# Two alternating tiles for the blocks to be inverted, in the room of a tile of ones and a score tile

## The chip, the cores and the metric

The kernel runs on one core of one Trainium2 chip. The metric is the device time in microseconds (us) of one execution; the time of a kernel is the median over its runs. A core has five engines that run side by side: TensorE (PE in the rows; its weight loads are PEld), VectorE (DVE), ScalarE (ACT), GpSimd (POOL) and SyncE (SP), whose queue issues most DMAs. Each takes its own instructions strictly in the order in which the kernel put them, and waits on semaphores for the others.

## The reference, cut to what matters

```python
for t in range(S):                                   # S = 768 steps, state [B=4, H=8, 40, 40]
    y[:, :, t] = einsum('bhd,bhde->bhe', rt, state)
    Sa = einsum('bhde,bhe->bhd', state, at)
    state = state * wt - einsum('bhd,bhe->bhde', Sa, bt) + einsum('bhd,bhe->bhde', vt, kt)
...
mixed = real(fft(fft(x, axis=1), axis=2)); u = x + mixed           # x: y as [4, 768, 320]
u = u + relu(norm(u) @ w_ch1) @ w_ch2                              # 1280 wide
u = u + (relu(u.T @ w_tok1) @ w_tok2).T                            # over the sequence, 256 wide
out = u + relu(u @ w_ch1') @ w_ch2'                                # 1536 wide
```

A recurrence over 768 steps of 32 heads comes first, then a Fourier mixing and three two-layer networks. The weights are held in 64 bits and are decoded to a high and a low part on the chip.

## The kernel before, in words

The recurrence is cut into 12 windows of 64 steps (`NSC=768//L`). For each window i these stages are built, each a method of `Attn`:

- `load`, `decay`: the decays `wS` come in; a backward scan on DVE writes `Q` (L262), a reciprocal writes column 0 of `D2` (L264), and a forward scan with `D2` writes `R` (L265). `Q` is one tile, `R` has five. The backward scan takes a second tile, `D1`, which is zero but for a column of ones and is written once, in `init`. `D2` is zero too, but for its column 0, which the reciprocal fills anew in each window. POOL (in the first windows DVE) then multiplies `bt` and `a` and copies the last column of `R` (L268).
- `kg`: matmuls of the scaled keys give `RT` (four tiles). The diagonal 32x32 blocks of `RT` go to DRAM (`Gd<-RT`) and come back with the blocks of heads on partitions (`N<-Gd`): the even window of a pair fills partitions 0 to 63 of `N`, the odd one 64 to 127. There is one tile `N`.
- `inv`: once for two windows, DVE inverts all 128 triangular blocks in some forty dependent steps from `N` into `Mt`, with `MT` as scratch: the first step is a copy of the diagonal band (L333), the last reads of `N` are the products for the off-diagonal half (L331, `pr<-N,MT`), and the last step is a transposed copy to `MT` (L353). `Mt` and `MT` go to DRAM (`Md`, `Ad`).
- `merge`: the inverses come back (`AT<-Ad`, four times `Mst<-Md` for each window), and PE joins the halves (`mg`, `mc`) into `Mst`.
- `kbts`, `pts`, `load2`, `load3`: transposes of `bt` and `R`, and loads of v and r.
- `chain`: the recurrence over windows. PE products `x` (L424) from `RT` and the state `LT`, copied to `bdX`; products `z` (L436) with the inverse `Mst`; products `s` (L448), from which DVE and POOL (L452, L454) form the next state.
- `outp`: the output of the window. Six score groups: `sc` matmuls (L486), a copy to one of four score tiles `sc[k%4]` with a triangle mask (on DVE for k = 0, 2, 4; on ACT and POOL else), and the `y` matmuls (L504, L508) from it.

`wdec`, `decode` and `job` decode weights beside this. `out_tile` closes the room of `wS`, `Q`, `D1`, `D2`, `N`, `Mt`, `MT` and others and opens the tile `X` in it, which the Fourier stage `fft` reads; `fft2` and the networks (`ch`, `tok`, `tok2`) follow.

No order is written by hand. Each operation is given to a planner (`Plan.op`) with an engine, a guessed cost and the keys it reads and writes; from the keys come its dependences (a write waits for earlier reads and writes of the key). `Plan.emit` walks the operations in guessed time and, on each engine, takes of those that are ready the one with the smallest due time. Due times come from the guessed costs of the followers and from `OFF`, a table of offsets by stage and by stage and window. So a change of tiles or offsets may give every engine and SP's queue another order. Where a PE operation begins later than PE is free, and the planner's count of columns of the last 3.41 us is under `FILL[1]`, `fill` puts `warm` matmuls (L52) into the gap, whose result nobody reads.

Of the kernel before, what the change touches and what calls it, by code (L numbers as in the profile page):

```python
# [15 lines left out]
ALU = mybir.AluOpType  # L16
# [3 lines left out]
NG,NH,D,L=11,33,40,64  # L20
# [3 lines left out]
NBT,NR,NA,NRT=4,5,2,4  # L24
# [155 lines left out]
class Attn:  # L180
    def __init__(s,tc,ident,A,xd,ctx,pctx,xstack,tstack,T1d,W):
        s.tc=tc; s.nc=nc=tc.nc; s.ident=ident; s.A=A; s.xd=xd; s.xstack=xstack; s.tstack=tstack; s.T1d=T1d; s.W=W; s.X=None
        s.late=ExitStack(); s.mid=ExitStack(); s.early=ExitStack()
        e=s.late.enter_context(tc.tile_pool(name="a_e",bufs=1,side="right"))
        c=ctx.enter_context(tc.tile_pool(name="a_c",bufs=1))
# [70 lines left out]
    def decay(s,i):  # L256

        nc=s.nc; P=s.P; W=NG*(L+1)
        w=s.wS[i%2].rearrange("p g t -> p (g t)"); Q=s.Q[0]; R=s.R[i%NR]; D1=s.D1.rearrange("p g t -> p (g t)")
        D2=s.D2[0]; a=s.a[i%NA]; bt=s.bt[i%NBT]  # L260
        kw,kR,ka=('wS',i%2),('R',i%NR),('a',i%NA)
        P.op('DVE',1.84,lambda: nc.vector.tensor_tensor_scan(out=Q[:,W-1::-1],data0=w[:,W-1::-1],data1=D1[:,W-1::-1],initial=1.0,op0=ALU.mult,op1=ALU.add),[kw,'D1','Qe'],['Q'])  # L262
        PL=view(Q,1,[L+1,NG],[1,1])
# [24 lines left out]
    def kg(s,i):  # L288
        nc=s.nc; P=s.P; RT=s.RT[i%NRT]; bt=s.bt[i%NBT]
        am,kam=(s.am,'am') if i!=1 else (s.rm,'rm')  # L290
# [18 lines left out]
        R=i//2  # L309
# [4 lines left out]
        x=i%2  # L314
        s.dma(s.N[64*x:64*x+64],s.Gd[R%2][x].rearrange("b n j t -> (b n) j t"),[('Gd',R%2,x,b) for b in range(2)],[('N',x)],.85)


    def inv(s,R):
        nc=s.nc; V=nc.vector; P=s.P
        N2=s.N.rearrange("p a b -> p (a b)"); M2=s.Mt.rearrange("p a b -> p (a b)"); T2=s.MT.rearrange("p a b -> p (a b)")  # L320
# [144 lines left out]
    def outp(s,i):  # L465
# [16 lines left out]
        for k in range(6):  # L482
            gs=(k,k+6) if k<5 else (k,); m=len(gs); hs=s.psum('m',[128,512],"sc"); ks=('ps',hs[0]); j=k%4; t=s.sc[j]
            def f(gs=gs,hs=hs):
# [95 lines left out]
    def plan(s):  # L580
# [25 lines left out]
BL=2.761166073747128  # L606
OFF={'chain': -53.3, 'dec2': -42.2, 'decay': -47.7, 'decode': -65.8, 'fft': 52.7, 'fft2': -1.1, 'inv': 6.1,
     'kbts': -59.8, 'kg': -24.1, 'load': 23.5, 'load2': -12.5, 'load3': 57.3, 'loada': 23.1, 'merge': 4.3,
     'mlp': 83.4, 'out_tile': 104.0, 'outp': -27.8, 'pad': 107.3, 'pts': -24.7, 'tok': -208.8, 'tok2': -94.1,
     'wdec': -17.2, ('chain', 0): 52.1, ('chain', 1): -108.0, ('chain', 10): -36.6, ('chain', 11): 111.0, ('chain', 2): 26.3, ('chain', 3): 24.5,  # L610
     ('chain', 4): -27.4, ('chain', 5): 26.9, ('chain', 6): -31.5, ('chain', 7): 39.7, ('chain', 8): -97.4, ('chain', 9): -149.0, ('dec2', 0): 44.3,
     ('decay', 0): -79.2, ('decay', 1): 225.9, ('decay', 10): 52.5, ('decay', 11): -192.4, ('decay', 2): -350.0, ('decay', 3): 97.8, ('decay', 4): -8.0,
     ('decay', 5): -93.2, ('decay', 6): -36.4, ('decay', 7): -67.6, ('decay', 8): -26.7, ('decay', 9): 92.1, ('decode', 0): -15.0, ('fft', 0): 16.4,
     ('fft', 1): -226.4, ('fft', 2): -45.0, ('fft', 3): -150.0, ('fft2', 0): 17.0, ('fft2', 1): -24.7, ('fft2', 2): 34.9, ('fft2', 3): -36.4,
     ('inv', 0): 29.0, ('inv', 1): -35.3, ('inv', 2): -129.2, ('inv', 3): 6.5, ('inv', 4): -75.1, ('inv', 5): -3.6, ('kbts', 0): 21.2,
     ('kbts', 1): -16.2, ('kbts', 10): 101.1, ('kbts', 11): 40.4, ('kbts', 2): -47.2, ('kbts', 3): -102.5, ('kbts', 4): -141.5, ('kbts', 5): 81.5,
     ('kbts', 6): -102.5, ('kbts', 7): -63.4, ('kbts', 8): 26.3, ('kbts', 9): -73.0, ('kg', 0): -9.0, ('kg', 1): -49.8, ('kg', 10): -36.2,
     ('kg', 11): -191.3, ('kg', 2): 37.3, ('kg', 3): 95.7, ('kg', 4): 190.6, ('kg', 5): 19.9, ('kg', 6): -18.3, ('kg', 7): -91.4,
     ('kg', 8): -12.7, ('kg', 9): 21.0, ('load', 0): -74.7, ('load', 1): -11.2, ('load', 10): -128.8, ('load', 11): 53.3, ('load', 2): -92.0,
     ('load', 3): -31.7, ('load', 4): -86.8, ('load', 5): -25.2, ('load', 6): -288.2, ('load', 7): -85.8, ('load', 8): 56.2, ('load', 9): 109.9,  # L620
# [9 lines left out]
     ('outp', 8): 1.7, ('outp', 9): -65.6, ('pad', 0): 58.5, ('pts', 0): 27.8, ('pts', 1): -33.5, ('pts', 10): -26.1, ('pts', 11): -101.8,  # L630
     ('pts', 2): -149.3, ('pts', 3): 24.6, ('pts', 4): -146.2, ('pts', 5): 12.1, ('pts', 6): -66.4, ('pts', 7): -19.1, ('pts', 8): 33.0,
     ('pts', 9): -40.2, ('tok', 0): -61.9, ('tok', 1): -97.3, ('tok', 2): -41.9, ('tok', 3): 162.9, ('tok2', 0): 278.2, ('tok2', 1): 127.9,
     ('tok2', 2): -107.6, ('tok2', 3): -16.7, ('wdec', 0): -7.2}
# [43 lines left out]
class Mlp:  # L677
# [354 lines left out]
D2=(-60.0,1.0)  # L1032
# [56 lines left out]
```

## Time and profile before

| | us |
|---|---|
| median of 3 runs | 1023.37 (1022.95 to 1035.03) |
| the profiled execution's own time | 1029.61 |
| its span, first to last instruction | 1027.9 |
| PE busy in the span | 993.2 (97%) |
| DVE, ACT, POOL busy | 635.6, 422.8, 339.8 |

The profile is of one execution. A row of `--windows` kind gives the busy time of each engine in a stretch and the granted TensorE clock as a share of full speed: 1.00 is 2.4 GHz, 0.50 is 1.2 GHz. A row of the timeline gives start, duration, engine, line and operation, with the idle time before it and what ended that in square brackets. PE's busy time holds the `warm` matmuls, and its matmuls are pipelined, so that a busy PE is not PE at its peak.

### The profile page before, as it was taken

The numbers are of one execution on the slowest core, as the hardware profiler recorded it, in microseconds if no ns is written. First come the engines' busy times: TensorE is split into PE (matmuls) and PEld (weight loads), VectorE is DVE, ScalarE is ACT, GpSimd is POOL, SyncE is SP. The second block draws the span as 40 slices with busy tenths as digits, with TensorE's granted clock in tenths as the row PEclk, the third lists the DMA queues.
The fourth block names the chain that finished last, engine by engine and source line by source line (L and its number), as shares of the span: only waits on it lengthen the run. The fifth ranks groups of instructions, "written<-read, shape, count | busy, mean of one in ns | idle before, by whom it ended". The sixth has DMA issues, their size and how long they took to land.

```text
span 1027.9 us, 24475 instructions
## 1 busy us (share of the span) xinstructions
PE 993.2 (97%) x10135; PEld 951.4 (93%) x10135; DVE 635.6 (62%) x1346; ACT 422.8 (41%) x870; POOL 339.8 (33%) x425
## 2 busy tenths in 40 slices
PE   8898999899999999899999999999999999999998
PEld 8897888787888988899999999999999999999998
DVE  7598589788978539797888885334432432332322
ACT  4256587686766755342343422223221221221221
POOL 8584377668754544302344434100000000000000
PEclk9999699999999999899999999999999999999999
DMA  9986596989877887822454545900000000000000
GB/s 209 196 169 149 132 210 144 183 183 218 185 177 163 229 236 217 276 66 68 146 158 158 166 142 162 377 1 1 1 20 1 20 1 20 20 1 20 20 21 19
DMA packets 140722, 125.51 MB, mean 122 GB/s; under 512 B 100867, under 2 KB 118275, under 8 KB 140483
## 3 DMA queue, kind: packets, MB, share of 16 engines
q1 hardware_dynamic: 135811, 100.29, 39.6%
q0 software_dynamic: 4800, 23.67, 6.7%
q8 instruction: 79, 1.29, 0.6%
q14 instruction: 32, 0.26, 0.1%
HBM read 85.40 MB, written 33.75 MB: 116 GB/s over the span
## 4 chain that ended last, share of the span: by engine, by line
PE 73%; DVE 14%; DMA 6%; issue 2%; POOL 2%; SPq 2%; ACT 1%; DVEq 0%; POOLq 0%; ACTq 0%
PE hps L917 22%; PE acc L907 21%; DVE pr L331 4%; PE warm L52 4%; PE sc L486 3%; PE mix L851 3%; PE psA L824 2%; PE kg L297 2%; PE t2ps L994 2%; PE tps L981 2%; DMA Mst<-Md 2%; PE y L508 2%; SPq L217 1%; PE trp L888 1%; PE x L424 1%
## 5 line engine op out<-in xcount | busy, mean ns | idle before, releaser
L920 DVE SCALAR_TENSOR_TENSOR hl<-hps,hh 128x384 fp32r<-128x384 f32 x176 | 97.8, 556 | 239.0 <-ACT hh L919 238.4
L919 ACT ACTIVATE hh<-hps 128x384 fp32r<-128x384 f32 x176 | 86.4, 491 | 306.9 <-PE hps L917 306.9
L917 PE MATMUL hps<-th,v 128*128 128x384 f32 x576 | 143.0, 338 | 0.0
L907 PE MATMUL acc<-v,hh 128*128 128x320 f32 x576 | 129.5, 311 | 0.0
L917 PE MATMUL hps<-th,W 128*128 128x384 f32 x480 | 119.7, 339 | 0.9 <-DVE th L893 0.6
L907 PE MATMUL acc<-W,hh 128*128 128x320 f32 x480 | 107.9, 311 | 0.0
L52 PE MATMUL warm<-ident 128*128 128x128 f32 x760 | 101.5, 288 | 5.4 <-DVE A L833 3.4
L917 PEld LDWEIGHTS hps<-th,v 128*128 128x128 f32 x576 | 103.8, 188 | 0.2
L52 PEld LDWEIGHTS warm<-ident 128*128 128x128 f32 x760 | 96.2, 202 | 6.6 <-issue 3.5
L907 PEld LDWEIGHTS acc<-v,hh 128*128 128x128 f32 x576 | 97.6, 188 | 0.0
L785 POOL TENSOR_TENSOR mda<-mda,mdh 128x320 f32<-128x320 f32 (+2 forms) x44 | 44.4, 1009 | 153.9 <-ACT mdh L782 111.0
L917 PEld LDWEIGHTS hps<-th,W 128*128 128x128 f32 x480 | 86.8, 188 | 2.5 <-DVE th L893 1.0
L907 PE MATMUL acc<-v,hl 128*128 128x320 f32 x288 | 89.0, 309 | 0.0
L907 PEld LDWEIGHTS acc<-W,hh 128*128 128x128 f32 x480 | 80.8, 188 | 0.0
L907 PE MATMUL acc<-W,hl 128*128 128x320 f32 x240 | 74.0, 308 | 0.0
L917 PE MATMUL hps<-tl,v 128*128 128x384 f32 x192 | 64.6, 337 | 0.0
L307 POOL TENSOR_SCALAR_AFFINE_SELECT RT<-RT 64x384 f32<-64x384 f32 x72 | 52.6, 756 | 33.7 <-ACT RT L219 32.3
L297 PE MATMUL kg<-am,bt 120*128 120x192 f32 x242 | 52.2, 352 | 8.0 <-issue 2.6
L486 PE MATMUL sc<-rm,VZd 120*128 120x192 f32 x264 | 57.0, 350 | 2.1 <-DMA VZd<-in_vR_dram 1.0
L907 PEld LDWEIGHTS acc<-v,hl 128*128 128x128 f32 x288 | 54.1, 188 | 0.0
L917 PE MATMUL hps<-tl,W 128*128 128x384 f32 x160 | 53.9, 337 | 0.0
L496 POOL TENSOR_SCALAR_AFFINE_SELECT sc<-sc 64x384 f32<-64x384 f32 (+1 forms) x72 | 44.0, 612 | 27.3 <-ACT sc L219 24.7
(175 smaller groups left out, 2090.7 us busy)
## 6 DMA issues: line engine op xcount, KB each, us to landing
bt<-in_bkR_dram SPq DMA_DIRECT2D x12, 660.0 KB
mdraw<-in_moe_w_ch_dram SPq DMA_DIRECT2D x22, 320.0 KB
wS<-in_wR_dram SPq DMA_DIRECT2D x12, 335.2 KB
a<-in_aR_dram SPq DMA_DIRECT2D x12, 335.2 KB
RT<-a SPq DMA_DIRECT2D x36, 111.7 KB
LT<-in_vT_dram SPq DMA_DIRECT2D x12, 330.0 KB
VZt<-in_vT_dram SPq DMA_DIRECT2D x12, 330.0 KB
r<-in_rR_dram SPq DMA_DIRECT2D x12, 330.0 KB
```

The lines of the kernel that those rows point to most:

```text
L52: for x in range(m): nc.tensor.matmul(t[:,128*(x%4):128*(x%4)+128],lhsT=ident,rhs=ident,start=True,stop=True)
L297: nc.tensor.matmul(ps[:,192*x:192*x+192],lhsT=bt[:,g+x].rearrange("p v t -> p (v t)"),rhs=am[:,:,g+x],start=True,stop=True)
L307: nc.gpsimd.affine_select(out=kv,in_=kv,pattern=[[0,3*m],[1,L]],compare_op=ALU.is_gt,fill=0.0,base=0,channel_multiplier=-1)
L331: P.op('DVE',.16+.0012*st[0]*shape[0],lambda: V.tensor_tensor(out=pr,in0=a,in1=b,op=ALU.mult),rd,[('pr',h)])
L486: for x,g in enumerate(gs): nc.tensor.matmul(ps[:,192*x:192*x+192],lhsT=VZd[:,g].rearrange("p v t -> p (v t)"),rhs=s.rm[:,:,g],start=True, ...
L496: nc.gpsimd.affine_select(out=o,in_=o,pattern=[[0,3*m],[1,L]],compare_op=ALU.is_gt,fill=0.0,base=0,channel_multiplier=-1)
L785: P.op('POOL',.06+d*.0028,lambda: nc.gpsimd.tensor_tensor(out=g("da").bitcast(F32),in0=g("da").bitcast(F32),in1=g("dh").bitcast(F32),op=AL ...
L851: nc.tensor.matmul(s.pst(h)[:,:320],lhsT=aa[:K,sl],rhs=T2[:K,tb],start=n==0,stop=n==7)
L907: nc.tensor.matmul(s.pst(acc[x]),lhsT=a[:,sl],rhs=t[w2][w][:,m],start=(m==0 and n==0),stop=(m==MT-1 and n==2))
L917: for n,(l,r) in enumerate(ops): nc.tensor.matmul(ps,lhsT=l,rhs=r,start=n==0,stop=n==7)
L919: s.act(384,lambda: nc.scalar.activation(out=t["hh"][z],in_=s.pst(h),func=AF.Relu),[kp],[('hh',z)],free=[h[0]])
L920: s.dve(.47,lambda: nc.vector.scalar_tensor_tensor(out=t["hl"][z],in0=s.pst(h),scalar=0.0,in1=t["hh"][z].bitcast(F32),op0=ALU.max,op1=ALU. ...
```

## The change

`D1` goes. The backward scan reads `D2` instead, and before it in each `decay` POOL sets the column 0 of `D2` to one: 12 small memsets, in place of one memset of a whole tile and one of a column in `init`. Since the reciprocal and the forward scan of a window use the same column, the memset of window i+1 waits for the forward scan of window i, and the backward scan of window i+1 waits for the memset. `N` becomes two tiles, used in turn by the pairs of windows (`R%2`), so that the loads of a pair no longer wait for the reads of the pair before. The score tiles become three (`k%3`). The offsets `OFF` are changed in about a third of their entries, and `FILL[1]` rises from 9558.7 to 10345.2. `Gd`, `Md`, `Ad` had two tiles each and keep them; `Mt` and `MT` stay single.

```diff
-        s.D1,=mk(e,1,[120,NG,L+1],"D1"); s.D2=mk(e,1,[120,NG,L+1],"D2")
+        s.D2=mk(e,1,[120,NG,L+1],"D2")
-        s.N,=mk(e,1,[128,32,32],"N"); s.Mt,=mk(e,1,[128,32,32],"Mt"); s.MT,=mk(e,1,[128,32,32],"MT")
+        s.N=mk(e,2,[128,32,32],"N"); s.Mt,=mk(e,1,[128,32,32],"Mt"); s.MT,=mk(e,1,[128,32,32],"MT")
-        s.ys,=mk(c,1,[128,720],"ys"); s.sc=mk(c,4,[128,6,L],"sc")
+        s.ys,=mk(c,1,[128,720],"ys"); s.sc=mk(c,3,[128,6,L],"sc")
...
     def init(s):
-        s.zero(s.D1,['D1'],.63); s.one(s.D1[:,:,0:1],['D1'])
...
     def decay(s,i):
-        P.op('DVE',1.84,lambda: nc.vector.tensor_tensor_scan(out=Q[:,W-1::-1],data0=w[:,W-1::-1],data1=D1[:,W-1::-1],...),[kw,'D1','Qe'],['Q'])
+        s.one(D2[:,:,0:1],['D2']); D1=D2.rearrange("p g t -> p (g t)")
+        P.op('DVE',1.84,lambda: nc.vector.tensor_tensor_scan(out=Q[:,W-1::-1],data0=w[:,W-1::-1],data1=D1[:,W-1::-1],...),[kw,'D2','Qe'],['Q'])
...
-        s.dma(s.N[64*x:64*x+64],s.Gd[R%2][x].rearrange("b n j t -> (b n) j t"),[('Gd',R%2,x,b) for b in range(2)],[('N',x)],.85)
+        s.dma(s.N[R%2][64*x:64*x+64],s.Gd[R%2][x].rearrange("b n j t -> (b n) j t"),[('Gd',R%2,x,b) for b in range(2)],[('N',R%2,x)],.85)
...
-        NK=[('N',0),('N',1)]
+        NK=[('N',R%2,0),('N',R%2,1)]
...
-            ...; ks=('ps',hs[0]); j=k%4; t=s.sc[j]
+            ...; ks=('ps',hs[0]); j=k%3; t=s.sc[j]
...
-OFF={'chain': -53.3, 'dec2': -42.2, 'decay': -47.7, 'decode': -65.8, 'fft': 52.7, 'fft2': -1.1, 'inv': 6.1,
+OFF={'chain': -53.3, 'dec2': -42.2, 'decay': -47.7, 'decode': -65.8, 'fft': 43.0, 'fft2': -1.1, 'inv': 24.4,
...
-     ('inv', 0): 29.0, ('inv', 1): -35.3, ('inv', 2): -129.2, ('inv', 3): 6.5, ('inv', 4): -75.1, ('inv', 5): -3.6, ('kbts', 0): 21.2,
+     ('inv', 0): 29.0, ('inv', 1): -35.3, ('inv', 2): -149.9, ('inv', 3): -17.3, ('inv', 4): -75.1, ('inv', 5): -3.6, ('kbts', 0): 21.2,
...
-FILL=(0.22,9558.7)
+FILL=(0.22,10345.2)
```

## Rows read from the trace of the kernel before

**Rows 1.** Busy time by stage: us, PE, PEld, DVE, ACT, POOL, clock, DMA share, GB/s.

```profile
0.00:445.00 445.00, 415.21 (x6409) 376.88 (x6410) 346.14 (x669) 270.35 (x529) 263.33 (x339) 0.96 0.81 193
445.00:1028.00 583.00, 577.95 (x3728) 574.54 (x3727) 289.43 (x678) 152.50 (x342) 76.50 (x86) 1.00 0.21 68
```

**Rows 2.** The same stages, the `warm` matmuls alone: PE and PEld busy.

```profile
0.00:445.00 445.00, 98.09 (x737) 93.07 (x738) 0.96 0.81 193
350.00:400.00 50.00, 10.98 (x78) 10.14 (x78) 0.97 0.92 260
```

**Rows 3.** Chain of waits near window 10: start, us, what.

```profile
346.96 1.09 PE x L424 x32
...
348.76 12.13 DMA Mst<-Md
...
366.10 1.26 PE z L436 x32
```

**Rows 4.** SP's queue in the same stretch, timeline.

```profile
348.76 0.96 SPq L217 DMA_DIRECT2D Mst<-Md  x2
356.52 0.35 SPq L778 DMA_DIRECT2D mdraw<-in_moe_w_ch_dram  x1
357.42 0.46 SPq L217 DMA_DIRECT2D Mst<-Md  x1
```

**Rows 5.** Busy time and clock around a fall of the clock, columns as rows 1.

```profile
100.00:105.00 5.00, 3.56 (x48) 2.92 (x48) 4.86 (x11) 0.71 (x2) 4.32 (x6) 0.79 0.78 190
105.00:120.00 15.00, 15.00 (x177) 12.76 (x178) 9.95 (x21) 5.96 (x11) 2.54 (x6) 0.50 0.49 139
```

**Rows 6.** POOL's groups by shape: busy us, mean ns, idle before.

```profile
L268 POOL COPY R<-Q 120x11 f32<-120x11 f32 x10 | 3.5, 349 | 2.5 <-DVE R L265 2.3
...
L221 POOL MEMSET D<- 120x715 f32 x2 | 1.4, 694 | 0.0
...
L223 POOL MEMSET D<- 120x11 f32 x1 | 0.1, 113 | 0.0
```

**Rows 7.** DVE timeline: the first backward scan, and the one that waited for POOL.

```profile
4.34 1.65 DVE L262 TENSOR_TENSOR_SCAN Q<-wS,D 120x715 f32<-120x715 f32 x1 [4.34 <-DMA wS<-in_wR_dram]
...
25.94 1.65 DVE L262 TENSOR_TENSOR_SCAN Q<-wS,D 120x715 f32<-120x715 f32 x1 [1.04 <-POOL R L268]
```

**Rows 8.** DVE timeline: first copies of inversions 1 and 5, end of inversion 4.

```profile
83.44 0.57 DVE L333 COPY Mt<-N 128x4 f32<-128x4 f32 x1 [3.48 <-DMA Ad<-MT]
...
271.93 1.15 DVE L331 TENSOR_TENSOR pr<-N,MT 128x512 f32<-128x512 f32 x1
...
284.03 1.38 DVE L353 COPY MT<-Mt 128x1024 f32<-128x1024 f32 x1
...
299.56 0.17 DVE L333 COPY Mt<-N 128x4 f32<-128x4 f32 x1 [1.66 <-DMA N<-Gd]
```

**Rows 9.** SP's queue: the loads of N for inversion 5.

```profile
273.82 0.48 SPq L217 DMA_DIRECT2D N<-Gd  x1
...
287.96 1.02 SPq L217 DMA_DIRECT2D Gd<-RT  x2
...
293.36 0.95 SPq L217 DMA_DIRECT2D N<-Gd  x1
```

**Rows 10.** PE timeline: scores and outputs of windows 2, 3 and 11.

```profile
162.98 0.55 PE L508 MATMUL y<-kbt,sc 128*64 128x40 f32 x12 [1.25 <-DVE sc L491]
...
189.51 1.57 PE L486 MATMUL sc<-rm,VZd 120*128 120x192 f32 x8
191.01 0.43 PE L504 MATMUL y<-Sbd,r 120*64 120x120 f32 x4
...
398.10 0.50 PE L508 MATMUL y<-kbt,sc 128*64 128x40 f32 x12
398.53 1.57 PE L486 MATMUL sc<-rm,VZd 120*128 120x192 f32 x8
```

More of the change, by code (lines that the diff above doesn't have):

```diff
@@ L258, in decay @@
         nc=s.nc; P=s.P; W=NG*(L+1)
-        w=s.wS[i%2].rearrange("p g t -> p (g t)"); Q=s.Q[0]; R=s.R[i%NR]; D1=s.D1.rearrange("p g t -> p (g t)")
+        w=s.wS[i%2].rearrange("p g t -> p (g t)"); Q=s.Q[0]; R=s.R[i%NR];
         D2=s.D2[0]; a=s.a[i%NA]; bt=s.bt[i%NBT]
         kw,kR,ka=('wS',i%2),('R',i%NR),('a',i%NA)
-        P.op('DVE',1.84,lambda: nc.vector.tensor_tensor_scan(out=Q[:,W-1::-1],data0=w[:,W-1::-1],data1=D1[:,W-1::-1],initial=1.0,op0=ALU.mult,op1=ALU.add),[kw,'D1','Qe'],['Q'])
+        s.one(D2[:,:,0:1],['D2']); D1=D2.rearrange("p g t -> p (g t)")
+        P.op('DVE',1.84,lambda: nc.vector.tensor_tensor_scan(out=Q[:,W-1::-1],data0=w[:,W-1::-1],data1=D1[:,W-1::-1],initial=1.0,op0=ALU.mult,op1=ALU.add),[kw,'D2','Qe'],['Q'])
         PL=view(Q,1,[L+1,NG],[1,1])
@@ L482, in outp @@
         for k in range(6):
-            gs=(k,k+6) if k<5 else (k,); m=len(gs); hs=s.psum('m',[128,512],"sc"); ks=('ps',hs[0]); j=k%4; t=s.sc[j]
+            gs=(k,k+6) if k<5 else (k,); m=len(gs); hs=s.psum('m',[128,512],"sc"); ks=('ps',hs[0]); j=k%3; t=s.sc[j]
             def f(gs=gs,hs=hs):
@@ L538, in out_tile @@
         nc=s.nc; P=s.P; f=XW//2
-        keys=['D1','Q','D2',('N',0),('N',1),'m8','Mt','MT','dec']+[(v,x) for v in ('t1','m16','pr') for x in range(2)]+[(v,x) for v in ('t2','m32') for x in (0,4,8,10,12,14)]+['mt1','mt2']+[('wS',x) for x in range(2)]+[('a',x) for x in range(NA)]+[('am',h) for h in range(3)]
+        keys=['Q','D2']+[('N',y,x) for y in range(2) for x in range(2)]+['m8','Mt','MT','dec']+[(v,x) for v in ('t1','m16','pr') for x in range(2)]+[(v,x) for v in ('t2','m32') for x in (0,4,8,10,12,14)]+['mt1','mt2']+[('wS',x) for x in range(2)]+[('a',x) for x in range(NA)]+[('am',h) for h in range(3)]
         def close():
@@ new lines @@
+OFF={'chain': -53.3, 'dec2': -42.2, 'decay': -47.7, 'decode': -65.8, 'fft': 43.0, 'fft2': -1.1, 'inv': 24.4,
+     'kbts': -59.8, 'kg': -24.1, 'load': 23.5, 'load2': -12.5, 'load3': 57.3, 'loada': 16.2, 'merge': 4.3,
+     'mlp': 107.2, 'out_tile': 91.3, 'outp': -27.8, 'pad': 107.3, 'pts': -18.5, 'tok': -208.8, 'tok2': -104.1,
+     'wdec': -17.2, ('chain', 0): 52.1, ('chain', 1): -108.0, ('chain', 10): -36.6, ('chain', 11): 111.0, ('chain', 2): 26.3, ('chain', 3): 9.5,
+     ('chain', 4): -112.3, ('chain', 5): 26.9, ('chain', 6): -31.5, ('chain', 7): 39.7, ('chain', 8): -97.4, ('chain', 9): -149.0, ('dec2', 0): 44.3,
+     ('decay', 0): -79.2, ('decay', 1): 225.9, ('decay', 10): 52.5, ('decay', 11): -201.9, ('decay', 2): -346.1, ('decay', 3): 117.7, ('decay', 4): -8.0,
+     ('decay', 5): -93.2, ('decay', 6): -36.4, ('decay', 7): -67.6, ('decay', 8): -26.7, ('decay', 9): 92.1, ('decode', 0): -15.0, ('fft', 0): 19.6,
+     ('fft', 1): -165.9, ('fft', 2): 8.1, ('fft', 3): -150.0, ('fft2', 0): 17.0, ('fft2', 1): -13.2, ('fft2', 2): 34.9, ('fft2', 3): -36.4,
+     ('inv', 0): 29.0, ('inv', 1): -35.3, ('inv', 2): -149.9, ('inv', 3): -17.3, ('inv', 4): -75.1, ('inv', 5): -3.6, ('kbts', 0): 21.2,
+     ('kbts', 1): -16.2, ('kbts', 10): 85.1, ('kbts', 11): 40.4, ('kbts', 2): -47.2, ('kbts', 3): -102.5, ('kbts', 4): -141.5, ('kbts', 5): 95.3,
+     ('kbts', 6): -85.7, ('kbts', 7): -63.6, ('kbts', 8): 26.3, ('kbts', 9): -73.0, ('kg', 0): -9.0, ('kg', 1): -49.8, ('kg', 10): -36.2,
+     ('kg', 11): -226.7, ('kg', 2): 37.3, ('kg', 3): 95.7, ('kg', 4): 190.6, ('kg', 5): 19.9, ('kg', 6): -18.3, ('kg', 7): -91.4,
+     ('kg', 8): -12.7, ('kg', 9): 21.0, ('load', 0): -74.7, ('load', 1): -11.2, ('load', 10): -159.5, ('load', 11): 53.3, ('load', 2): -92.0,
+     ('load', 3): -31.7, ('load', 4): -86.8, ('load', 5): -25.2, ('load', 6): -288.2, ('load', 7): -85.8, ('load', 8): 37.5, ('load', 9): 109.9,
[3 rows of a table added]
+     ('load3', 7): -46.5, ('load3', 8): -92.2, ('load3', 9): -13.4, ('loada', 0): 57.4, ('loada', 1): -86.3, ('loada', 10): 32.3, ('loada', 11): -119.3,
+     ('loada', 2): -61.5, ('loada', 3): 267.5, ('loada', 4): -79.6, ('loada', 5): -1.2, ('loada', 6): 150.5, ('loada', 7): -45.8, ('loada', 8): 31.0,
@@ L630 @@
[L630 to L633, printed above, removed]
+     ('mlp', 1): 36.8, ('mlp', 2): 93.4, ('mlp', 3): 142.9, ('out_tile', None): -52.6, ('outp', 0): -149.2, ('outp', 1): 6.5, ('outp', 10): 13.8,
@@ new lines @@
+     ('outp', 11): -78.8, ('outp', 2): 15.1, ('outp', 3): 117.2, ('outp', 4): 18.4, ('outp', 5): 52.8, ('outp', 6): 0.8, ('outp', 7): 31.2,
+     ('outp', 8): 1.7, ('outp', 9): -25.6, ('pad', 0): 58.5, ('pts', 0): 27.8, ('pts', 1): -33.5, ('pts', 10): -26.1, ('pts', 11): -138.2,
+     ('pts', 2): -149.3, ('pts', 3): 24.6, ('pts', 4): -146.2, ('pts', 5): 12.1, ('pts', 6): -66.4, ('pts', 7): -4.5, ('pts', 8): 33.0,
+     ('pts', 9): -40.2, ('tok', 0): -61.9, ('tok', 1): -119.1, ('tok', 2): -10.0, ('tok', 3): 162.9, ('tok2', 0): 278.2, ('tok2', 1): 127.9,
@@ L634 @@
+     ('tok2', 2): -55.3, ('tok2', 3): -16.7, ('wdec', 0): -7.2}
 PH=0.0
-FILL=(0.22,9558.7)
+FILL=(0.22,10345.2)
 RL=(0.0,0.0,10.0,14.0,30.0)
```

18 lines of the change are left out of this document (1 added, 17 removed), and 6 rows, old and new, of the table OFF.

## The prediction, made before the changed kernel was timed

> **What bounds the kernel now.** I first read the busy time of the two stages. After 445 us PE is busy 577.95 of 583 us at clock 1.00 [rows 1]: the networks are bound by PE's own work, which the change leaves as it is, and only some 5 us of gaps are left there. Before 445 us PE is busy 415.21 us, but 98.09 of these are `warm` matmuls [rows 1, 2], so about 317 us of real work stand in 445. No engine is full there; that stage ends when the last window of the recurrence has come through. So a microsecond saved on the way to window 11 is a microsecond at the end, and one saved beside it is nothing.
>
> Next I read the chain of waits where it leaves PE for long. The longest piece is in window 10: its `x` matmuls end at 348.05, its `z` matmuls start at 366.10, and 12.13 us between them are a wait for `Mst<-Md`, the inverse of pair 5 [rows 3]. SP's queue shows why it is so long: after two pieces of `Mst` at 348.76 the queue stands until 356.52 at a load of raw weights, and the next piece of `Mst` goes out behind that load at 357.42 [rows 4]. The two pieces end issuing at 348.76 + 0.96 = 349.72, so 357.42 - 349.72 = 7.70 us are lost to the order of the queue.
>
> Then the clock. From 105 to 120 us PE is busy all 15 us at 0.50, that is 1.2 GHz, after a stretch in which it was busy 3.56 of 5 us [rows 5]. The same work at 2.4 GHz would take about half: at most 7.5 us lie there.
>
> **The change part by part.** All is summed against the profiled execution, 1029.61 us; that is 6.24 above the median of 1023.37, and I carry differences over to the median unchanged.
>
> *The tile of ones goes from `init`.* One memset of a whole tile (694 ns) and one of a column (113 ns) [rows 6] leave POOL before 4.34 us. The first backward scan was released by the load of `wS` [rows 7], not by POOL. I count 0; the other end is -0.8.
>
> *Twelve column memsets on POOL, each before a backward scan.* Each has the shape of the 113 ns one; the copy `R<-Q` of the same shape took 349 ns in the middle of the kernel [rows 6]. The new waits are on the forward scan of the window before and on the memset. The first is not new: the backward scan overwrites `Q`, which POOL's copy L268 reads after that forward scan. So the memset lies beside a copy that was waited for already, and one scan is seen to have waited for that copy, 1.04 us [rows 7]. Queued behind a waiting memset on POOL are the multiplications of `bt` and the masks of other windows; DVE's queue behind the scan holds the inversion. If the memset sat on the path in all twelve windows it would be 12 x 0.35 = 4.2 us; if it lies beside the copy, 0. I take 0.5, near the lower end, because only one scan waited at all.
>
> *Two tiles `N`.* No DMA is added; the twelve loads may only go earlier. What waited for `N` before? For inversion 5 the load of the even half left SP at 273.82, behind the last read of `N` by inversion 4, which ended at 271.93 + 1.15 = 273.08 [rows 8, 9]: that is the wait that goes. But the odd half left at 293.36, behind `Gd<-RT` of its own window at 287.96, and the inversion began at 299.56, released by that load [rows 8, 9]. The even half had by then been issued for 25 us. So the second tile frees a load that nobody waited for. Inversion 1 began behind `Ad<-MT`, that is behind the single `Mt` and `MT` [rows 8], which stay single. What is late next is in both cases what was late before. Direct gain 0.
>
> The Trainium skill (page "Trainium Kernel Development and Optimization", section Best Practices) says to double-buffer for performance, so that transfers lie beside compute. By that rule the load of inversion 5 would be hidden behind inversion 4 as a whole; the trace shows a load that waits for its source, not for its buffer, so the rule's gain is a rival here and not in the sum.
>
> From both sides: 0 if the odd half keeps its time, and at most the time from the end of inversion 4, 284.03 + 1.38 = 285.41, to 299.56 [rows 8], 14.15 us, if the planner uses the freedom to bring the odd window's `kg` forward so far that DVE goes from one inversion to the next. I take 0, since both rows name the source.
>
> *Three score tiles.* With four, PE could do the scores k = 0 to 3 before the first `y`; window 3 does (scores at 189.51, first `y` at 191.01 [rows 10]). With three, score 3 must come behind the first `y`, which needs tile 0 copied and masked. PE has waited for a score tile before: 1.25 us [rows 10]. One more such place in each of 12 windows is at most 12 x 1.25 = 15 us, at least 0 where PE has other work. In the last window the fourth score already stands behind the third `y` (398.10 and 398.53 [rows 10]), so the window that sets the end pays nothing; in the others the 98 us of `warm` matmuls show that PE has room. I take 1.0, nearest to 0.
>
> *A new order.* The offsets, the keys and the `FILL` threshold change, so every queue is planned anew. The two accidents above, 7.7 us at SP's queue and 7.5 us at half clock, belong to the old order, not to the work. A new order will have accidents of its own; I count half of these two as gone, -(7.7 + 7.5)/2 = -7.6. The ends are -15.2 (both gone, none new) and +7.5 (both stay and one like the half-clock stretch is added). The higher threshold means more `warm` matmuls in PE's gaps; PE's gaps hold them, so they cost nothing where the gap was real, and where PE's next operation comes earlier than planned, each is in the way for its 0.13 us (98.09 us by 737).
>
> Sum: 0 + 0.5 + 0 + 1.0 - 7.6 = -6.1. So 1029.61 - 6.1 = 1023.5 for an execution like the profiled one, and 1023.37 - 6.1 = 1017.3 for the median; I say 1017.
>
> **The rivals.**
>
> *Nothing but a shuffle.* The second tile frees nothing that was waited for, and the new order has as many accidents as the old. For it: `Mt`, `MT` and `Gd<-RT` are as before. Against it: the 7.70 us in SP's queue is a rare thing, the longest piece of the chain. Time: 1023.37 + 1.5 = 1025, say 1021 to 1027.
>
> *The inversions close up.* The planner, no longer held by `N`, brings the pairs' odd windows forward; DVE goes from inversion 4 straight to 5, window 10 finds its inverse waiting. For it: window 10 waits 18 us between `x` and `z`, and 10.98 us of `warm` matmuls stand between 350 and 400 [rows 2, 3], so there is room to close. Against it: the odd half waits for `Gd<-RT`. Time: 1023.37 - 14.15 + 1.5 = 1011, say 1003 to 1012. This is the time by the rule of double buffers.
>
> *Slower by the score ring.* Place: `outp` of the inner windows, where score 3 now stands behind the first `y`. It decides from the point where PE has no other operation ready while tile 0 is masked. If that is so in half the windows, 6 x 1.25 = 7.5 us, and the accidents stay: 1023.37 + 7.5 = 1031, say 1027 to 1040.
>
> **How the numbers follow.** Forecast (1012 to 1021) 0.45; shuffle 0.22; inversions close up 0.18; score ring 0.15. The range 1005 to 1030 takes in most of each neighbour: it leaves out perhaps 0.05 below and 0.09 above. Two per cent is 20.5 us, about what a measurement of this kernel can tell from no change; below 1002.9 I need the closing up and the new order's full gain together, 0.06; above 1043.8 the score ring in every window, 0.03; within, 0.91.
>
> **What would show it.** Right: `Mst<-Md` before the `z` of window 10 is several us shorter than 12.13 in the chain, no 15 us stretch at clock 0.50, the inversions still released by `N<-Gd` of the odd half, `Gd<-RT` just before it; the networks' stage is 583 us within 2. Wrong: inversion 5 begins within 3 us of the end of inversion 4 (the second rival); PE waits for score tiles add up to over 5 us (the third); a backward scan waits for the memset by more than 1 us; the stage before the networks ends at 445 again (the first); or the networks themselves take another time, which no step here foresees.

## The result, and the profile after

The changed kernel takes 1035.97 us, the median of 20 runs (1028.5 to 1043.02); the kernel before, run beside it, 1027.88 (median of 20, 1019.97 to 1045.93). The ratio of the runs is 1.0077, with a 95% interval of [1.0048, 1.0107]: slower by some 8 us, where 6 us less were forecast. The prediction's 1017 is missed, and so is its range (1005 to 1030). Of the 19 us between 1017 and 1035.97, 4.5 are the base alone (1023.37 of 3 runs, 1027.88 of 20). Medians here are of all runs, while a ratio leaves out runs in which the chip was in its slower state, so that a ratio need not be the quotient of the two medians beside it.

The profiled execution took 1040.14 us, 10.5 more than that of before; its span is 1038.4. Busy time by stage, columns as [rows 1], cut where the first matmul of the networks (`hps`) begins: at 446.6 before, at 454.0 now.

```profile
0.00:454.00 454.00, 424.73 (x6463) 384.35 (x6463) 350.60 (x671) 271.29 (x532) 264.83 (x349) 0.95 0.79 189
454.00:1038.00 584.00, 577.98 (x3726) 576.14 (x3724) 290.79 (x676) 151.45 (x339) 76.57 (x86) 1.00 0.21 68
```

The `warm` matmuls alone, as [rows 2]:

```profile
0.00:454.00 454.00, 106.31 (x790) 99.38 (x790) 0.95 0.79 189
454.00:1038.00 584.00, 3.27 (x23) 2.87 (x21) 1.00 0.21 68
```

So the recurrence ends 7.4 us later and the networks take 3.1 us more (584.4 for 581.3). Of these 3.1, 2.0 are one wait, which no step of the prediction foresaw: engine, line, what was waited for, us, times, longest.

```profile
PE acc L907 <- DVE X L930: 2.0, 1, 2.0
```

The stretch of [rows 5] that ran at 1.2 GHz runs at 2.4 GHz now. But other stretches of this execution fell to 1.2 GHz in whole or in part, two of them shown here (us, PE, PEld, DVE, ACT, POOL, clock):

```profile
105.00:120.00 15.00, 15.00 (x264) 13.32 (x263) 14.03 (x28) 9.82 (x20) 8.42 (x13) 1.00 0.53 140
...
320.00:335.00 15.00, 13.68 (x172) 11.72 (x170) 8.46 (x19) 5.25 (x11) 4.53 (x6) 0.66 0.36 110
370.00:380.00 10.00, 10.00 (x185) 9.45 (x182) 4.06 (x8) 5.01 (x11) 5.96 (x7) 0.52 0.92 259
```

SP's queue in window 10, as [rows 4]: four pieces of `Mst` now go out ahead of the load of raw weights, the last two from 352.32 on, where the last of before went out at 357.42.

```profile
349.09 1.52 SPq L217 DMA_DIRECT2D Mst<-Md  x2
352.32 1.09 SPq L217 DMA_DIRECT2D Mst<-Md  x2
353.61 0.35 SPq L778 DMA_DIRECT2D mdraw<-in_moe_w_ch_dram  x1
```

And yet `z` of that window starts at 366.57 (366.10 in [rows 3]); PE's timeline shows what it does instead of starting sooner:

```profile
358.22 1.20 PE L372 MATMUL mg<-AT,B 32*32 32x32 f32 x64
...
362.40 0.95 PE L382 MATMUL mc<-Mst,T 32*32 32x32 f32 x48
...
365.18 1.06 PE L52 MATMUL warm<-ident 128*128 128x128 f32 x8
...
366.57 0.84 PE L436 MATMUL z<-bdX,Mst 128*64 128x80 f32 x17
```

PE does other work until `mc`, which joins the halves of `Mst`, and does not wait for a piece there.

The inversions stand as the prediction said. Inversion 5, as [rows 8], is still released by the load of its odd half, and that load goes out behind `Gd<-RT` of its window, as [rows 9], a few us sooner than before (291.85 for 293.36):

```profile
285.51 1.05 DVE L353 COPY MT<-Mt 128x1024 f32<-128x1024 f32 x1
...
297.31 0.55 DVE L333 COPY Mt<-N 128x4 f32<-128x4 f32 x1 [0.41 <-DMA N<-Gd]
```

```profile
274.15 0.47 SPq L217 DMA_DIRECT2D N<-Gd  x1
...
287.32 0.93 SPq L217 DMA_DIRECT2D Gd<-RT  x2
...
291.85 0.87 SPq L217 DMA_DIRECT2D N<-Gd  x1
```

One backward scan waits for its memset, for as long as it waited for the copy in [rows 7]; the twelve memsets take 116 ns each, against 113 in [rows 6]. Over 1 us of such a wait was one of the prediction's signs of being wrong; what it costs is measured below (`share_scans`).

```profile
26.21 1.65 DVE L262 TENSOR_TENSOR_SCAN Q<-wS,D 120x715 f32<-120x715 f32 x1 [1.09 <-POOL D L223]
```

### The profile page after: what moved, and what is told of

It reads as the page before. It is cut to its first block, busy times and chain, and to the rows that moved or that the text cites. A ratio compares the mean times of both kernels' runs of the same rounds, so it can differ in the third digit from the quotient of the medians.

```text
span 1038.4 us, 24635 instructions
## 1 busy us (share of the span) xinstructions
PE 1002.7 (97%) x10185; PEld 960.5 (92%) x10185; DVE 641.4 (62%) x1346; ACT 422.7 (41%) x870; POOL 341.4 (33%) x435
## 4 chain that ended last, share of the span: by engine, by line
PE 56%; DVE 4%; DMA 1%; issue 1%; ACT 0%; SPq 0%; DVEq 0%; ACTq 0%
PE hps L917 23%; PE acc L907 22%; PE mix L851 3%; PE t2ps L994 2%; PE tps L981 2%; PE psA L824 2%; PE trp L888 1%; PE warm L52 1%; DVE Xl L812 1%; DMA X<-xd 1%; DVE mdt L784 0%; DMA mdraw<-in_moe_w_ch_dram 0%; DVE mda L781 0%; DVE un L872 0%; DVE mdt L780 0%
## 5 line engine op out<-in xcount | busy, mean ns | idle before, releaser
L52 PE MATMUL warm<-ident 128*128 128x128 f32 x810 | 109.6, 289 | 6.6 <-DVE A L832 4.3
L52 PEld LDWEIGHTS warm<-ident 128*128 128x128 f32 x810 | 102.3, 201 | 8.1 <-issue 4.4
L486 PE MATMUL sc<-rm,VZd 120*128 120x192 f32 x264 | 59.3, 356 | 0.0
L307 POOL TENSOR_SCALAR_AFFINE_SELECT RT<-RT 64x384 f32<-64x384 f32 x72 | 50.5, 725 | 17.2 <-ACT RT L219 15.9
L297 PE MATMUL kg<-am,bt 120*128 120x192 f32 x242 | 50.0, 342 | 3.9 <-issue 2.7
```

The lines of the kernel that those rows point to most:

```text
L52: for x in range(m): nc.tensor.matmul(t[:,128*(x%4):128*(x%4)+128],lhsT=ident,rhs=ident,start=True,stop=True)
L297: nc.tensor.matmul(ps[:,192*x:192*x+192],lhsT=bt[:,g+x].rearrange("p v t -> p (v t)"),rhs=am[:,:,g+x],start=True,stop=True)
L307: nc.gpsimd.affine_select(out=kv,in_=kv,pattern=[[0,3*m],[1,L]],compare_op=ALU.is_gt,fill=0.0,base=0,channel_multiplier=-1)
L486: for x,g in enumerate(gs): nc.tensor.matmul(ps[:,192*x:192*x+192],lhsT=VZd[:,g].rearrange("p v t -> p (v t)"),rhs=s.rm[:,:,g],start=True, ...
```

## The experiments

Each ratio below is to the kernel before, run beside it on the same chip. Several kernels keep one kernel's tiles and take another's order. They replace the planner's choice by a recorded list: of the operations whose dependences are met, the one that stands first in the list goes next. With its own list the kernel before issues on every engine what it issued without.

```diff
-            best=None
-            ... the choice by guessed times and due times
+            o=min((o for c in cand.values() for o in c if psready(o) is not None),key=lambda o: pos[o.idx])
```

### Tiles or order

`tiles_only`: the changed kernel's tiles, twelve memsets included, with the list of before.

> The changed tiles (no tile of ones, two N, three score tiles) and the 12 column memsets, with every operation in the order of the kernel before: each queue takes the operation that comes first in the old order among those whose dependences are met, so only the fourth score of a window moves behind the first y where it stood ahead of it. Theory 'order' (the tiles cost nothing, the re-planned queues cost the time): ratio to the kernel before 0.997 to 1.003, that is within 3 us, and window 11 ends within 3 us of before. Theory 'tiles' (the waits that the memsets and the score ring add cost the time): ratio 1.006 to 1.010, 6 to 10 us, with waits of PE for score tiles or of the backward scans for POOL in the trace.

1039.47 us for 1025.66, ratio 1.0158 [1.0095, 1.0221]. With nothing re-planned the tiles cost 16 us, twice what the whole change costs.

`order_only`: the tiles of before, with the list of the changed kernel and its `FILL`.

> The tiles of the kernel before, with every operation in the order of the changed kernel (its offsets and its warm-up threshold are in that order). Theory 'order': ratio 1.005 to 1.011, 5 to 11 us slower than before, with half-clock stretches after 250 us where the changed kernel has them. Theory 'tiles': ratio 0.997 to 1.003.

1030.65 us for 1025.66, ratio 1.0059 [1.0022, 1.0096]. The new order costs 6 us by itself. So both terms have the sign that the prediction's rivals gave them, and they do not add up: 1.0158 and 1.0059 make 1.022, and the changed kernel is at 1.0077. Put differently, on top of the new order the tiles cost 1.0077 - 1.0059, some 2 us, less than the intervals can tell from none.

`offsets_only` and `tiles_replanned` exchange the offsets and `FILL` alone and let the planner plan anew.

```diff
 # offsets_only: the kernel before with the changed kernel's tables
-OFF={... 'fft': 52.7, 'inv': 6.1, ...};  FILL=(0.22,9558.7)
+OFF={... 'fft': 43.0, 'inv': 24.4, ...}; FILL=(0.22,10345.2)
 # tiles_replanned: the changed kernel with the tables of before (the reverse)
```

> The kernel before with the new offsets and the new warm-up threshold alone, planned anew. Theory 'order': slower, as offsets that were set with other tiles give one more order among many; 1.003 to 1.015. Theory 'tiles': 0.997 to 1.003, since the offsets alone do no harm.

> The changed tiles with the old offsets and the old warm-up threshold, planned anew. Theory 'order': any re-planning moves the time by up to 1 per cent either way, so 0.995 to 1.015, and the stretch that loses time is not the same as in the changed kernel. Theory 'tiles': 1.006 to 1.010, with the same waits as in the changed kernel.

1059.06 us, ratio 1.0301 [1.0241, 1.0361], and 1054.21 us, ratio 1.0297 [1.0243, 1.035]. Each table suits only the tiles that it came with: without its own, the kernel before loses 3.0% and the changed kernel 2.2% (1.0297 for 1.0077). The offsets of the change, 48 of 185 entries, are no detail of it. Two thirds of the one loss and half of the other stand in the networks, which the planner now fills: they take 602.6 us in `offsets_only` for 581.3 before, with 155 `warm` matmuls for 20, and 594.7 in `tiles_replanned` for 584.4 in the changed kernel, with 111 for 23.

### Which tile

`ring3`: the kernel before with its list, and three score tiles. `share_scans`: its list, four score tiles, and the shared scan tile with its memsets. `share_ring5`: as `share_scans`, with five score tiles, and the fifth score issued earlier in nine of twelve windows.

```diff
 # ring3
-... s.sc=mk(c,4,[128,6,L],"sc")   ...   j=k%4
+... s.sc=mk(c,3,[128,6,L],"sc")   ...   j=k%3
 # share_scans: of the change the edits of D1, init, decay and out_tile, no others
 # share_ring5: these, and
+... s.sc=mk(c,5,[128,6,L],"sc")   ...   j=k%5
```

> The kernel before in its own order, with three score tiles for four and nothing else changed. Theory 'score ring': in an order planned for four tiles the copy of score 3 waits until the first y have read tile 0, and that is most of the 11 to 16 us that all new tiles together cost in this order: +8 to +14 us, 1.008 to 1.014 of before, and the waits of ACT's sc copies rise from 20.3 us before 445 towards 36.5. Rival 'shared scan tile': the twelve memsets and the shared tile carry it, and this is 1.000 to 1.003. Rival 'second N': the same, 1.000 to 1.003.

> The kernel before in its own order, four score tiles, one N; only the tile of ones goes, with twelve column memsets on POOL ahead of the backward scans. Theory 'score ring' (the ring alone is the price of the tiles): 0 to +2 us, 0.999 to 1.003 of before, the backward scans released by the memsets at a few places for under 1.5 us each. Rival 'shared scan tile': +4 to +10 us, 1.004 to 1.010.

> The kernel before's order with the tile of ones gone (twelve memsets) and its room given to a fifth score tile; the fifth score of each window is issued behind the fourth, ahead of what followed. Theory 'score ring': if a fourth tile is worth 13 to 16 us, a fifth is worth something of the same sign: 0.990 to 0.998 of before. Rival 'four are enough': with two PSUM banks for scores the fifth waits there, and it is 0.999 to 1.005.

`ring3`: 1042.26 us for 1028.19, ratio 1.0156 [1.0111, 1.0201]. `share_scans`: 1027.76 for 1028.37, 1.0001 [0.9966, 1.0035]. `share_ring5`: 1025.88 for 1028.37, 1.0005 [0.9973, 1.0038]. The score ring alone is the price of the tiles: `tiles_only` (1.0158) is `ring3` (1.0156) with the shared scan tile and the second `N` added, and no price of these two shows. For the shared scan tile `share_scans` bounds it to some 3.5 us; the second `N` was not run alone, and the difference of two ratios, each known to 0.0045 or 0.006, leaves it several us either way. No gain of a fifth tile shows either: of this ring the fourth tile counts.

The order of PE's queue shows what the ring does. The scores s0 to s5 and the outputs y0 to y5 of one window, as PE takes them:

```
window 3, before:   s1 s0 s3 s2 y0 y1 s4 s5 y2 y3 y4 y5
window 3, changed:  s1 s0 s2 y0 y1 s3 y2 s4 s5 y3 y4 y5
```

Before, the fourth score stands ahead of y0 in ten of twelve windows; changed, and in `ring3`, in none. It is the planner that puts it there: in `outp` the score matmul itself carries the key of the tile that its copy will fill (`('sc',j,0)`), so with three tiles the fourth one is issued behind y0, though it writes only PSUM. Three tiles in which the copy alone waits were not tried.

The price falls in the recurrence: the first network matmul of `ring3` begins at 461.8, 15.2 us later than before, and its networks take no longer (580.2 us for 581.3). The wait does not show on PE, whose `y` matmuls stand idle for score tiles 1.6 us in the changed kernel (2.3 before) and in `ring3` not at all: `warm` matmuls and other work stand in front of the waiting instruction. It shows on ACT, which copies scores. ACT's waits for them before 445 us, one row each of the kernel before, `ring3` and the changed kernel (total us, times, longest):

```profile
ACT sc L219 <- PE sc L486: 20.3, 16, 6.0
```

```profile
ACT sc L219 <- PE sc L486: 38.1, 22, 7.6
```

```profile
ACT sc L219 <- PE sc L486: 26.4, 23, 3.5
```

In the old order the three tiles nearly double ACT's wait; the new order, planned for three, brings it most of the way back. That fits the small price of the tiles there, but how much of ACT's wait is paid in time was not measured.

For `share_scans` the wait that the prediction named for the memsets is there, 11.6 us in eight places, and no cost of it shows in the time (1.0001):

```profile
DVE Q L262 <- POOL D L223: 11.6, 8, 4.4
```

### The two accidents of the old order

The prediction counted 7.7 us for SP's queue in window 10 and 7.5 us for the clock, and half of them as a gain. `mst_first` is the kernel before with one SP instruction moved:

```diff
 SP's queue, window 10
 Mst<-Md x2
-mdraw<-in_moe_w_ch_dram
-m11h<-mdh
 Mst<-Md
+mdraw<-in_moe_w_ch_dram
+m11h<-mdh
```

> The kernel before with one change, on SP's queue alone: in window 10 the last piece of Mst<-Md is issued ahead of the load of raw weights that held it from 349.72 to 356.52. Theory 'head of line' (the prediction's step): z of window 10 starts up to 7.7 us sooner behind its x, 18 to 20 us become 11 to 13, and all of it reaches the end: -4 to -8 us, 0.992 to 0.996 of before. Rival 'late anyway': the load of weights and what hangs on it come later instead, or z waits for other pieces: x to z stays over 16 us and the ratio is 0.999 to 1.003.

1030.47 us for 1028.37, ratio 1.0004 [0.9965, 1.0044]. The last piece of `Mst` now leaves SP in one row with two others, from 351.71 to 353.70, while the load of weights stands until 359.72:

```profile
351.71 1.99 SPq L217 DMA_DIRECT2D Mst<-Md  x3
359.72 0.35 SPq L778 DMA_DIRECT2D mdraw<-in_moe_w_ch_dram  x1
```

PE hardly takes it up. Its queue still has transposes and `warm` matmuls in front of `mc`, and `z` starts at 366.25:

```profile
359.10 1.73 PE L52 MATMUL warm<-ident 128*128 128x128 f32 x14
...
362.72 0.44 PE L382 MATMUL mc<-Mst,T 32*32 32x32 f32 x16
...
366.25 1.33 PE L436 MATMUL z<-bdX,Mst 128*64 128x80 f32 x32
```

From the start of `x` to that of `z` in window 10 it is 17.5 us (348.77 to 366.25), for 20.5 in the profile of before, 18.5 in that of `order_net`, which has the same order there, and 17.8 in the changed kernel: 1 to 3 us shorter, not 7.7. At the end no gain shows, and the interval allows at most 3.6 us. The trace of before had the reason. This is PE in window 10 there:

```profile
358.97 0.63 PE L394 MATMUL kbt<-ident,bt 120*128 120x120 f32 x4
359.53 0.24 PE L382 MATMUL mc<-Mst,T 32*32 32x32 f32 x2
360.94 0.43 PE L382 MATMUL mc<-Mst,T 32*32 32x32 f32 x14 [1.17 <-DMA Mst<-Md]
```

PE comes to `mc` at 359.53, 14.0 us after its first `x` (345.57), and then stands idle for the piece of `Mst` only 1.17 us. In `mst_first` it comes to `mc` 14.0 us after its first `x` too (348.77, 362.72), and does not wait. The 12.13 us of [rows 3] were the last wait to end, not the only one: with the DMA early, PE's own queue was as late.

The clock's stretch is no property of the order. Five profiled kernels here issue the same instructions up to 195 us. The stretch of [rows 5] is at half clock or nearly so in three of them (0.50, 0.50, 0.54) and at 2.4 GHz in `order_w6to11` and, as here, in `order_net`, both below:

```profile
105.00:120.00 15.00, 14.80 (x294) 12.82 (x293) 11.81 (x25) 11.81 (x24) 7.53 (x11) 1.00 0.75 195
```

`order_net` is identical to before up to its first network matmul, and reaches it at 438.5, before at 446.6: 8.1 us between two executions of the same instructions.

### Where in the order

Three kernels with the tiles and `FILL` of before take the new list for one part each: up to the first `z` of window 6, from there to the first network matmul, and from there on.

```diff
-pos: list of before
+order_w0to5:  new list to z of window 6, then before's
+order_w6to11: before's to z of window 6, the new to the first hps, then before's
+order_net:    before's to the first hps, then the new
```

> The kernel before, with its own tiles; every operation up to the first z of window 6 is issued in the changed kernel's order, all later ones in the order of before. Theory 'late windows': the new order loses its time in windows 6 to 11, so this is 1.000 to 1.003 of before (0 to +3 us): in the changed kernel z of window 6 began 1.2 us later than before (259.0 for 257.8). Rival 'early windows': the new order loses early (z of window 5 at 227.8 to 229.5 for 223.6) and never gets it back: +4 to +6 us, 1.004 to 1.006. Rival 'networks': 1.000.

> The kernel before, with its own tiles; operations up to the first z of window 6 and those from the first network matmul on in the order of before, the ones between in the changed kernel's order. Theory 'late windows': +5 to +7 us, 1.005 to 1.007 of before, the first network matmul 5 to 7 us later than 446.6, behind the masks of the weights on DVE in window 11. Rivals 'early windows' and 'networks': 0 to +2, 1.000 to 1.002.

> The kernel before, with its own tiles; the order of the changed kernel only from the first network matmul on. Theories 'late windows' and 'early windows': 0 to +1 us, 1.000 to 1.001 of before. Rival 'networks': the new order of acc and hps matmuls opens gaps in a stage that PE bounds (584.4 us in the changed kernel for 581.3): +3 to +6 us, 1.003 to 1.006.

`order_w0to5`: 1029.24 us for 1028.19, ratio 1.0025 [0.9991, 1.0059]. `order_w6to11`: 1037.44, 1.011 [1.0061, 1.0159]. `order_net`: 1037.86, 1.0095 [1.0054, 1.0137]. None of the three theories gives these three numbers. Together they would be 1.023, far over the 1.0059 of the whole list, so a seam between two lists seems to cost by itself. For `order_net` the seam can be seen. Its networks take 589.0 us for 581.3, with 80 `warm` matmuls in them, where before and the changed kernel have 20 and 23 (rows of `order_net`, then of before: busy us, mean ns, idle):

```profile
L52 PE MATMUL warm<-ident 128*128 128x128 f32 x80 | 10.5, 275 | 0.0
```

```profile
L52 PE MATMUL warm<-ident 128*128 128x128 f32 x20 | 2.9, 274 | 0.0
```

Their 10.5 us for 2.9 are 7.6 of the 7.7 us of difference, 10.5/80 = 0.13 us for each. So this run says what a `warm` matmul costs in a stage that PE bounds, and hardly anything of the new order there.

Against the profile of before, every kernel with the new order from the start was ahead at `z` of window 4 and had lost half of its lead or more by `z` of window 6. Two more lists tried that stretch alone:

```diff
-pos: new list                          (order_w5_back)
+pos: new list, before's between the z of windows 4 and 6
-pos: list of before                    (order_w5_only)
+pos: list of before, the new between the z of windows 4 and 6
```

> The kernel before's tiles in the changed kernel's order, except that the operations between the first z of window 4 and that of window 6 are issued as before. Theory 'window 5' (the new order loses there and nowhere else before the networks): z of window 4 to z of window 6 takes 60 to 62 us for 66 to 68, and the run is 0.998 to 1.001 of before. Rival 'given back': the stretch is shorter, the later windows wait for their inverses as before, and it is 1.004 to 1.009.

> The kernel before, with the changed kernel's order only between the first z of window 4 and that of window 6. Theory 'window 5': 66 to 68 us for 60 to 62 there, and +5 to +7 us, 1.005 to 1.007 of before. Rival 'given back': the late z of window 5 is caught up behind the next inverse, 0.999 to 1.003.

`order_w5_back`: 1033.71 us for 1027.99, ratio 1.0054 [1.0024, 1.0083]. `order_w5_only`: 1031.21, 1.0017 [0.9983, 1.0051]. The theory of window 5 falls. First starts of `z`, from the traces:

| | window 4 | window 5 | window 6 | 4 to 6 | window 11 |
|---|---|---|---|---|---|
| before | 196.1 | 223.6 | 257.8 | 61.7 | 383.9 |
| changed | 192.2 | 229.5 | 259.0 | 66.8 | 391.3 |
| order_only | 188.7 | 227.8 | 256.4 | 67.7 | 378.1 |
| order_w5_back | 187.8 | 216.8 | 254.1 | 66.3 | 376.6 |
| order_net (order of before up to here) | 191.0 | 218.3 | 250.8 | 59.9 | 376.1 |

With the old stretch put back, window 5 comes 11 us sooner (216.8 for 227.8) and window 6 only 2: what its `z` follows is not window 5. The rows are of single executions whose mean granted clock differs (0.982 before, 0.979 changed, 0.993 `order_only` and `order_w5_back`, 0.988 `order_net`), so a few us between two of them say little.

Last, the scores alone: the new list, in which each window's scores, copies, masks and outputs stand among themselves as before, with four tiles.

```diff
-window 3: s1 s0 s2 y0 y1 s3 y2 s4 s5 y3 y4 y5
+window 3: s1 s0 s3 s2 y0 y1 s4 s5 y2 y3 y4 y5
```

> The kernel before's tiles in the changed kernel's order, but in every window the scores, their copies and masks, and the y matmuls stand among themselves as before: four scores ahead of the first y in ten windows for none. Theory 'the ring is in the order': the 6 to 8 us that the changed order costs with four score tiles are the fourth score behind the first y; they come back, 0.998 to 1.002 of before. Rival 'other queues': the cost is elsewhere in the new order and stays, 1.005 to 1.009.

1040.46 us for 1028.37, ratio 1.0142 [1.009, 1.0193]: slower still, though ACT's wait for scores falls to 16.9 us. The early fourth score has no worth of its own that could be put into any order: forcing the other pattern in costs 1.6% in the old order (`ring3`) and 0.8% in the new (1.0142 for 1.0059). That each order is built around its own pattern would explain both, but is not shown; this run also has 932 `warm` matmuls, 120 more than `order_only`.

### The warm matmuls

The slower kernels have more `warm` matmuls: 760 before, 810 changed, 846 in `ring3` (though `share_ring5`, which is not slower, has 828, and `order_w6to11`, which is, 758). Cause, or sign of the waits? Four kernels scale each stretch of them, all queues as they were:

```diff
+            s.wsum=getattr(s,"wsum",0.0)+m*380/423; m=int(s.wsum+1e-6); s.wsum-=m   # ring3_fewer_warm
             if not DRY: s.filler(*b,m)
```

> The kernel before, every queue in its order, but each stretch of warm matmuls made longer by a ninth: 846 warm matmuls for 760, as with three score tiles. 86 at 0.13 us are 11 us of PE. Theory 'in the way': they delay the operations behind them, +8 to +11 us, 1.008 to 1.011 of before, less what a clock that falls less gives back. Rival 'sign of waits': PE stands idle there anyway, -4 to +3 us, 0.996 to 1.003.

> Three score tiles in the order of before (1.0156 of it with 846 warm matmuls), with each stretch of warm matmuls cut so that there are 760, as before. Theory 'in the way': most of the 13 to 16 us go, 1.002 to 1.007. Rival 'sign of waits': the queue behind the fourth score waits as long with PE idle, 1.011 to 1.018.

> The kernel before's tiles in the changed kernel's order (1.0059 with 812 warm matmuls), cut to 760. Theory 'in the way': 52 fewer at 0.13 us are 6.8 us, 0.999 to 1.002 of before. Rival 'sign of waits': 1.005 to 1.009.

> The changed kernel (1.0077 with 810 warm matmuls), each stretch of warm matmuls cut so that there are 760. Theory 'in the way': 0.999 to 1.003 of before. Rival 'sign of waits': 1.006 to 1.010, or more where the clock falls oftener.

Each is scaled to the count of another kernel: 846 in `more_warm`, 760 in the rest. Against 1027.19 us: `more_warm` 1032.15, ratio 1.0036 [1.0006, 1.0065]; `ring3_fewer_warm` 1036.9, 1.0116 [1.0077, 1.0155]; `order_fewer_warm` 1032.47, 1.0058 [1.0034, 1.0083]; `after_fewer_warm` 1032.34, 1.0064 [1.0032, 1.0095]. The 86 more of `more_warm` take 11 us of PE and cost 3.7 us, a third. Without the additional ones the new order costs what it did (1.0058 for 1.0059), the changed kernel hardly less (1.0064 for 1.0077), and three score tiles still 1.2%. So cutting them gives little of the time back, or none.

That is not yet to say that they cost nothing, for the granted clock differs too. In the 103 runs of the kernel before that the ratios use, and that have their clock on record, 0.01 less of mean granted clock goes with 7.0 us more (a straight line through them, correlation -0.83). By this line the excess of each version over the kernel before at the same mean clock can be estimated. The line is rough: the changed kernel's own 20 runs give 9.3 us for 0.01.

| | mean clock | slower by the ratio, us | at the same clock, us (estimate) |
|---|---|---|---|
| order_only | 0.987 | 6.1 | 7 |
| order_fewer_warm | 0.981 | 6.0 | 4 |
| changed | 0.983 | 7.9 | 8 |
| after_fewer_warm | 0.980 | 6.6 | 4.5 |
| ring3 | 0.982 | 16.0 | 13 |
| ring3_fewer_warm | 0.980 | 11.9 | 8.5 |
| order_w0to5 | 0.987 | 2.6 | 5 |
| order_w6to11 | 0.976 | 11.3 | 4 |

Three things follow from it, as estimates. The changed kernel is not slower by its clock: its mean of 0.983 is that of these 103 runs too. The additional `warm` matmuls cost some 3 to 5 us at the same clock; the runs without them have a lower mean clock, which takes back all of that in the new order with four tiles and less of it in the other two. And neither of the two parts of the new order before the networks looks free: the ratio of `order_w0to5` is low with a high clock, that of `order_w6to11` high with a low one.

No version beat the kernel before: `share_scans`, `share_ring5`, `mst_first`, `order_w0to5` and `order_w5_only` cannot be told from it by their ratios, all others are slower.

## Why the prediction was wrong, point by point

**The step that failed: "a new order", -7.6.** It measured +6 (1.0059), near the other end that the prediction had kept (+7.5). The step had two parts, and both failed. The hold in SP's queue did belong to the old order, and it did go; but its 7.70 us were no gain, since PE's own queue was as late: PE stood idle for that piece 1.17 us, and taking the hold away alone gave a ratio of 1.0004 (`mst_first`). The stretch at 1.2 GHz does not belong to the old order: it comes and goes between executions of the same instructions, and the profiled execution of the changed kernel had falls of its own later, at 320 and at 370 us. The length of a wait was taken for a gain with no row that showed when PE would have been ready without it. The prediction did say that a new order has accidents of its own, yet its -7.6 holds nothing for them; the runs show a cost of 6 us.

The signs of being right did not bear on the time: no wait of PE for `Mst<-Md` is left in window 10, no stretch of 15 us at half clock, and the inversions are released as foretold, in a kernel that is slower.

**Three score tiles, +1.0.** In the old order this is 16 us (`ring3`), at the end that the prediction named as the worst (12 x 1.25 = 15) and did not take. The argument that 98 us of `warm` matmuls show room on PE was wrong: with three tiles the recurrence grew by 15 us, and the planner put 86 more `warm` matmuls into it. On top of the new order the term is small, some 2 us, as taken; that the order was planned around three tiles would explain it.

**The rival that came true** is the third, slower by the score ring, at 1031 for a base of 1023.37; the ratio 1.0077 on that base gives 1031.2. Its place is only half right: PE's waits for score tiles did not pass 5 us in the changed kernel, the mark the prediction set, and the price sits in the order. So the time is right by luck: the rival had 7.5 us for the ring and nothing for the order, and the runs have some 2 and 6.

**What held.** The memsets: 0.5 taken, a ratio of 1.0001 measured. The second `N`: 0 taken; `tiles_only` and `ring3` differ by 0.0002, and inversions are still released by the odd half, as the rows of before had said. The Trainium skill (page "Trainium Kernel Development and Optimization", section Best Practices) says to double-buffer for performance, so that transfers lie beside compute. By that rule a gain was to be had here; none shows, and in the trace the load of the odd half goes out behind its source, `Gd<-RT`. The higher `FILL` threshold: with the order of before it changes no instruction at all. That an added `warm` matmul costs nothing where the gap is real, and 0.13 us where not, fits the 3.7 us that 11 us of them cost.

**Not foreseen:** the networks' 3.1 us, 2.0 of them the wait of `acc` for DVE.

**What stays open.** Why the new order costs 6 us with four tiles. Cutting the additional `warm` matmuls, putting window 5 back and putting the fourth score back each left the time where it was or raised it, and no one part of the list is seen to carry the cost. That it is the price of planning around three tiles, half of what three tiles cost without planning, fits these runs but is argued, not shown. Offsets fitted to four score tiles in place of three, the rest of the change kept, would tell; beside two tiles `N` the room for that is short by 0.34 kB per partition, and it was not tried.

## What to carry to other kernels

A wait that is last in the chain of waits is worth only the distance to the next one, so before counting it as a gain, read when the consumer's own queue would have been ready without it, and how long the consumer itself stood idle: here 1.17 us of 12.13. Shortening a ring of small tiles is not made free by filler on the engine in front of it: look for the wait on the engines that fill and empty the ring. And where the order comes from a planner with fitted offsets, try the tiles under the old order and the old tiles under the new one; here the tiles alone cost twice what both together did. Where runs differ by their clock, set the clock beside each ratio before reading small differences.

## What was not expected of the hardware

The clock does not fall at the same places in each execution: identical instructions ended their first stage 8.1 us apart (438.5 and 446.6), and in one set of runs the kernel before took 1016.54 us at a mean granted clock of 0.993 and 1030.04 at 0.977. A single profile's half-clock stretch is therefore no term of a sum. In the networks, where PE is busy 576 of 581 us, 60 more `warm` matmuls cost their full 0.13 us each (`order_net`); spread over the whole kernel, nearly all in the recurrence, 86 more cost a third of that (3.7 us of 11, with an interval of 0.6 to 6.7).
